# A twelfth cell and eight more key blocks of V 4 in the 15 KB that GpSimd's DMA scratch held

## The chip, the cores and the metric

The kernel runs on one core of one Trainium2 chip. The metric is the device time of one execution in microseconds, a median over runs. One core has a matrix engine (TensorE, PE in the profile, with PEld for its weight loads), VectorE (DVE), ScalarE (ACT), GpSimd (POOL), and SyncE (SP), which here only issues loads. Sixteen DMA engines move data from device memory (HBM) to the on-chip memory of 128 partitions (SBUF). TensorE writes to a second, smaller memory (PSUM).

## The reference: one token through two layers

One token of width 640 passes twice through the same pair of blocks: attention A over a cache of keys and values, and a small MLP B. Both passes read the same weights and, above all, the same two caches.

```python
x = A_x                                                    # [1, 1, 640]
for layer in range(2):
    x = x + A(layernorm(x), k_cache, v_cache, wq, wo)
    x = x + B(layernorm(x), w1, w2, w3, w4)

def A(x, k_cache, v_cache, wq, wo):                        # 32 heads of width 192
    q = (x @ wq) per head
    k, v = the last 4096 keys and values of the 32768 in each head's cache
    p = softmax(q @ k.T * 192 ** -0.5)
    return concat over heads (p @ v) @ wo

def B(x, w1, w2, w3, w4):
    x1 = x + (h = gelu(layernorm(x) @ w1), shifted by one or two tokens in four channel groups) @ w2
    return x1 + gelu(layernorm(x1) @ w3) @ w4
```

With one token every shift brings in zeros, so that w1 and w2 give nothing and B is the part with w3 and w4. All is bf16. One head's window of keys is 4096 x 192 x 2 B = 1536 KB, and so is that of its values: 32 heads, K and V, two layers make up nearly all that is moved.

## The kernel before

**Cells.** SBUF holds NCELL = 11 cells of 12,288 B in each of 128 partitions (FREE = 6144 bf16, 1536 KB in all). A cell takes one head's K window, one head's V window, a chunk of wo (four heads), or most of w3 or w4. `take` (L116) hands out the cell that was given back longest ago, `give` (L121) puts one at the end of the list. wq stays in SBUF for good. One order of loads, written out by `layer_stream` (L205) for each layer, is issued on SP's queue; `need` (L249) issues the loads up to the one that is asked for. A load waits on the queue until the cell that it was given is free, and all loads behind it wait too.

**One head.** K arrives with keys on partitions. VectorE transposes it in 32 x 32 blocks, in four quarters (`transpose_quart`, L360, the instruction is at L377), into a cell called the area, of which each quarter is reused; then TensorE computes the scores from the quarters (`scores`, L443, matmul at L453). When four heads (a group) have their scores, the softmax follows (`softmax_steps`, L473: part_max at L478 to recip at L533). Then P.V of the four heads, one after the other (`pv`, L560, matmul at L569), each followed by a transpose into o_sb (L576) and a fold (`o_fold`, L578). While one group is in P.V, the next one's K is transposed and its scores are computed. Layer 0 goes through the groups from the last (heads 28 to 31) to the first (0 to 3), layer 1 from the first to the last.

**What layer 0 keeps for layer 1.** Since both layers read the same caches, what stays on the chip needn't be loaded again:

- transposed keys of heads 0 to 6 (NKEEP = 7), each in a cell of its own taken at L369; layer 1 uses them without a load or a transpose, and gives the cell back after the head's scores (L664);
- V of head 3 (VC) in its cell;
- V of head 2 (VP): 20 of its 32 blocks wait in PSUM, into which and out of which VectorE transposes them (`v_words`, L550, at L558), the others in the cell of wo's chunk 0, which is kept too. In layer 1 head 2's V takes a cell, but has no load;
- of V of head 4 (VX) the last NKX = 6 of 32 key blocks, in a tile of their own, kx. A key block is 192 columns: one key per partition. In layer 1 the first 33 partitions of kx serve as row space after P.V of head 4 (L352, cleared at L853).

**Around the change of layers.** At the end of layer 0 seven cells hold kept keys, one V 3 and one wo chunk 0; two are left, through which w3 and w4 pass and then V 0 and V 1 of layer 1. The next cells come free only as layer 1 uses up kept heads: scores of heads 0 to 3 (L707), then those of 4 to 6 (L748), then the softmax of the first group, P.V of head 3, and only then the transposes and scores of head 7, whose K is the third load of layer 1. The load order of layer 1 is V 0, V 1, K 7, V 2 (no transfer), K 8, V 4, K 9, V 5, K 10 and so on. V 2's place in it is set at L233: behind the K of head NKEEP.

**The scratch.** The first 16 KB of each partition are set aside by the framework for descriptors of GpSimd's DMAs. The kernel issues no DMA from GpSimd.

The functions with the line numbers that the profile uses:

Of the kernel before, what the change touches and what calls it, by code (L numbers as in the profile page):

```python
# [8 lines left out]
BF16 = mybir.dt.bfloat16  # L9
# [8 lines left out]
P = 128  # L18
# [12 lines left out]

NJ4, NGK, NM = 4, 8, 4


@with_exitstack
def kernel(
# [12 lines left out]
    out: bass.AP,  # L49
):  # L50
    nc = tc.nc
    _, _, D = A_x.shape
    _, H, Sk, Dh = A_k_cache.shape
    W = min(4096, max(256, Sk // 4))
# [8 lines left out]
    QH = 4  # L63
# [5 lines left out]
    FREE = NT * QUART  # L69
# [2 lines left out]
    s0 = Sk - W  # L72

    NA = Dh // 32
    NKX = 6
    NKEEP, NCELL = 7, 11
    WARM = 4

    VC, VP, VX, VW, VN = 3, 2, 4, 20 * Dh // 2, NKX * Dh
    assert NA * D + FREE - 2 * VW <= FREE

    W3C, W4C = FREE // F, FREE // D
# [1 line left out]
    GROUPS = [[list(range(h, h + QH)) for h in range(0, H, QH)] for _ in range(2)]  # L86
    GROUPS[0].reverse()

    head = ctx.enter_context(tc.tile_pool(name="head", bufs=1))
    fixed = ctx.enter_context(tc.tile_pool(name="fixed", bufs=1))  # L90
    cells = ctx.enter_context(tc.tile_pool(name="cells", bufs=1))
# [11 lines left out]
        name=nc.get_next_instruction_name(), act_func_set_id=ACT_TABLE_SET, ins=[], outs=[]))  # L103
# [1 line left out]
    wq_sb = fixed.tile([P, ND, HD], BF16, name="wq_sb")  # L105
    wx_sb = fixed.tile([P, (ND - W3C) * F + (NF - W4C) * D], BF16, name="wx_sb")

    kx = fixed.tile([P, VN], BF16, name="kx")

# [4 lines left out]
    def take(key):  # L116
        i = free.popleft()
        cell_of[key] = i
        return cells.tile([P, FREE], BF16, tag=f"cell{i}", name=f"cell{i}")

    def give(key):  # L121
        free.append(cell_of.pop(key))
# [7 lines left out]
    def load_k(layer, h):  # L130
        t = take(("k", layer, h))
        nc.sync.dma_start(t[:], A_k_cache[0, h, s0:Sk, :].rearrange("(p j) d -> p (j d)", p=P))
        return t

    def load_v(layer, h):
        t = take(("v", layer, h))
        src = A_v_cache[0, h, s0:Sk, :].rearrange("(p j) d -> p (j d)", p=P)
        cut = (2 * VW,) if h == VP else (FREE - VN,) if h == VX else ()
        if h in GROUPS[layer][-1][-1 - layer:]:
            cut = FREE // 2,  # L140
        i = 0
        for e in cut + (FREE,):
            kept_v = h == VP or h == VX and i > 0
            if layer == 0 or not kept_v:
                nc.sync.dma_start(v_pair(t, h, i, e - i), src[:, i:e])
            i = e
        return t

    def v_pair(V, h, i, n):

        if h == VP and i >= 2 * VW:
            V, i = loaded["wo", 0, 0], i - 2 * VW + NA * D
        elif h == VX and i >= FREE - VN:
            V, i = kx, i - (FREE - VN)
        return V[:, i:i + n]

    def load_wq(layer, kc):
# [3 lines left out]
    def load_wo(layer, c):  # L161
        t = take(("wo", layer, c))
        src = A_wo[c * QC:(c + 1) * QC, :].rearrange("(p c) n -> p (c n)", c=NA)
        parts = {NG - 2: (3, 3), NG - 1: (3, 2, 1)}.get(c, (NA,)) if layer == 1 else (NA,)
        i = 0
        for n in parts:
            nc.sync.dma_start(t[:, i * D:(i + n) * D], src[:, i * D:(i + n) * D])
            i += n
        return t
# [13 lines left out]
    def load_w4(layer):  # L183
# [17 lines left out]
        return blocks  # L201

    LOADERS = {"x": load_x, "k": load_k, "v": load_v, "wq": load_wq, "wo": load_wo, "w3": load_w3, "w4": load_w4}

    def layer_stream(layer):  # L205
        groups = GROUPS[layer]
        seq, later = [], []

        def k_item(hh):
            if layer == 0 or hh >= NKEEP:  # L210
                seq.append(("k", layer, hh))

        def v_item(hh):
            if (layer, hh) == (1, VC):
                return
            if (layer, hh) == (1, VP):
                later.append(("v", layer, hh))
                return
            seq.append(("v", layer, hh))

        if layer == 0:
            for hh in groups[0]:
                k_item(hh)
        for gi, cur in enumerate(groups):
            nxt = list(groups[gi + 1]) if gi + 1 < len(groups) else []
            late = gi + 2 >= len(groups)
            for i, hh in enumerate(cur):
                if nxt:
                    k_item(nxt.pop(0))
                if nxt and late and i == 2:  # L230
                    k_item(nxt.pop(0))
                v_item(hh)
                if later and seq[-1] == ("k", layer, NKEEP):  # L233
                    seq.append(later.pop())
                if layer == 0 and gi + 1 == len(groups) and i < 2:
                    seq.append(("wo", layer, groups[gi + i - 1][0] // QH))
            if gi + 2 < len(groups) and gi >= layer:
                seq.append(("wo", layer, cur[0] // QH))
        if layer == 1:
            for g in groups[-2:]:  # L240
                seq.append(("wo", layer, g[0] // QH))
        seq.append(("w3", layer))
        seq.append(("w4", layer))
        return seq

    stream = [("wq", 0, 0), ("x",)] + [("wq", 0, kc) for kc in range(1, ND)] + layer_stream(0) + layer_stream(1)
    pos = [0]

# [311 lines left out]
    def pv(layer, h, hq, PT, mid=None):  # L560
        V = need("v", layer, h)
        if (layer, h) == (0, VP):
            v_words(0)
        NB = NJ4 * NGK // 2
        for i in range(NB):
            if mid is not None and i == NB // 2:
                mid()
            r = 32 * (i % 4)
            nc.tensor.matmul(O_ps[r:r + 2, :], lhsT=PT[:, hq, 2 * i:2 * i + 2],  # L569
                             rhs=v_pair(V, h, 2 * i * Dh, 2 * Dh), start=(i < 4), stop=(i >= NB - 4))  # L570
        if (layer, h) == (0, VC):
            loaded["v", 1, h] = V
            cell_of["v", 1, h] = cell_of.pop(("v", 0, h))
        else:
            give(("v", layer, h))
        nc.vector.transpose(o_sb[:], O_ps.rearrange("p (e a c) -> p e c a", e=2, c=NA))  # L576
# [426 lines left out]
```

## Time and profile before

| what | value |
|---|---|
| median of 3 runs | 519.34 us (519.17 to 519.5) |
| profiled execution, first to last instruction (span) | 517.8 us |
| median less span | 1.5 us |
| moved by DMA | 217.08 MB, 419 GB/s over the span |
| busy share: PE, DVE, ACT | 62%, 57%, 9% |
| K loads / whole V loads (1536 KB each) | 57 / 56 |
| mean granted TensorE clock | 0.697 of full speed |

Of the profiled execution the page gives the span alone: the time from its first instruction to its last. What an execution takes beside that isn't shown; the difference to the median of the runs is the estimate in the table.

How to read the lines in what follows: the page cuts the span into 40 slices of 12.9 us; a digit is the busy share in tenths, and GB/s is what the DMA engines moved in the slice. A timeline line has start and duration in us, engine, line of the kernel, operation, output <- inputs, shape, count of merged instructions, and in brackets the idle time of the engine before it and what ended that. SPq is SyncE's queue; its DMA lines are issues, and the data land later. A line of waits has the engine, its line and who ended the wait, then us in total, times, and the longest. A table of windows has a stretch, its length, the busy time of PE, PEld, DVE, ACT and POOL with counts, the granted TensorE clock, the DMA engines' busy share and GB/s.

### The profile page before, as it was taken

The numbers are of one execution on the slowest core, as the hardware profiler recorded it, in microseconds if no ns is written. First come the engines' busy times: TensorE is split into PE (matmuls) and PEld (weight loads), VectorE is DVE, ScalarE is ACT, GpSimd is POOL, SyncE is SP. The second block draws the span as 40 slices with busy tenths as digits, with TensorE's granted clock in tenths as the row PEclk, the third lists the DMA queues.
The fourth block names the chain that finished last, engine by engine and source line by source line (L and its number), as shares of the span: only waits on it lengthen the run. The fifth ranks groups of instructions, "written<-read, shape, count | busy, mean of one in ns | idle before, by whom it ended". The sixth has DMA issues, their size and how long they took to land.

```text
span 517.8 us, 9464 instructions
## 1 busy us (share of the span) xinstructions
PE 321.8 (62%) x4084; PEld 190.0 (37%) x4084; DVE 294.9 (57%) x591; ACT 48.9 (9%) x173; POOL 4.0 (1%) x16
## 2 busy tenths in 40 slices
PE   1057656666655655767755866668666667648665
PEld 0024333333332433434333634334333334425334
DVE  2067767575584764666624264756576766664722
ACT  1000101010010100001011001001010101001011
POOL 2000000000000000000000000000000000000000
PEclk9997778565585776677665567657787865776855
DMA  8999999999999999999999999999999999999996
GB/s 348 432 429 426 429 428 429 429 429 424 433 426 427 432 425 428 429 427 428 426 420 401 377 424 430 428 424 427 433 428 427 429 429 427 426 432 427 427 417 250
DMA packets 24093, 217.08 MB, mean 419 GB/s; under 512 B 2548, under 2 KB 3060, under 8 KB 8692
## 3 DMA queue, kind: packets, MB, share of 16 engines
q1 hardware_dynamic: 24052, 216.48, 99.0%
q8 instruction: 32, 0.52, 0.4%
q14 instruction: 9, 0.07, 0.0%
HBM read 216.47 MB, written 0.00 MB: 418 GB/s over the span
## 4 chain that ended last, share of the span: by engine, by line
DMA 50%; PE 23%; DVE 22%; issue 3%; ACT 1%; SPq 1%; DVEq 0%; ACTq 0%
DMA cell<-in_A_k_cache_dram 28%; DVE cell L377 16%; DMA cell<-in_A_v_cache_dram 16%; PE ST_ps L453 10%; PE O_ps L569 7%; DMA cell<-in_A_wo_dram 4%; DVE o_sb L576 2%; DMA cell<-in_B_w_dram 2%; DVE pm L478 1%; PE nb_ps L501 1%; DVE o_sb L512 1%; ACT o_sb L507 1%; PE l_ps L528 1%; PE PT_ps L523 1%; PE qT_ps L407 1%
## 5 line engine op out<-in xcount | busy, mean ns | idle before, releaser
L453 PE MATMUL ST_ps<-cell,Qblk 128*16 128x256 bf16 x1536 | 163.8, 383 | 108.2 <-DVE cell L377 70.1
L377 DVE STREAM_TRANSPOSE cell<-cell 128x768 uint32<-128x768 uint32 x228 | 204.0, 944 | 14.6 <-DMA cell<-in_A_k_cache_dram 14.3
L453 PEld LDWEIGHTS <-Qblk 128*16 128x16 bf16 x1536 | 85.8, 112 | 178.2 <-issue 151.0
L569 PE MATMUL O_ps<-cell,PT 128*2 128x384 bf16 x1018 | 98.7, 456 | 7.5 <-DMA cell<-in_A_v_cache_dram 5.5
L576 DVE STREAM_TRANSPOSE o_sb<-O_ps 128x384 f32<-128x384 f32 x64 | 37.1, 580 | 109.5 <-PE O_ps L569 109.4
L569 PEld LDWEIGHTS <-PT 128*2 128x2 bf16 x1024 | 45.6, 100 | 21.2 <-issue 11.4
L512 DVE STREAM_TRANSPOSE o_sb<-o_sb 128x256 bf16<-128x256 bf16 x16 | 7.1, 445 | 33.4 <-ACT o_sb L507 22.5
L584 ACT ACTIVATE oT<-oT_ps,rl 32x6 bf16<-32x6 f32 x40 | 10.3, 257 | 162.9 <-PE oT_ps L583 156.7
L583 PE MATMUL oT_ps<-o_sb,Lq 128*32 128x6 f32 x160 | 13.8, 195 | 10.4 <-DVE o_sb L576 9.9
L583 PEld LDWEIGHTS oT_ps<-o_sb,Lq 128*32 128x32 f32 x160 | 13.1, 145 | 19.4 <-issue 15.6
L589 ACT ACTIVATE oT<-oT_ps,rl 32x6 bf16<-32x6 f32 x24 | 6.2, 257 | 107.1 <-PE ST_ps L453 86.8
L407 PE MATMUL qT_ps<-xc,wq_sb 128*128 128x1 bf16 x210 | 7.2, 165 | 13.1 <-DMA wq_sb<-in_A_wq_dram 12.2
L523 PE MATMUL PT_ps<-o_sb,Eq 128*32 128x32 bf16 x256 | 7.2, 237 | 9.2 <-DVE o_sb L512 4.1
L421 DVE TENSOR_TENSOR Xq<-qT_ps,maskq 128x24 bf16<-128x24 f32 (+1 forms) x18 | 2.9, 159 | 17.4 <-PE qT_ps L407 17.4
L523 PEld LDWEIGHTS <-Eq 128*32 128x32 bf16 x256 | 5.4, 109 | 19.3 <-issue 19.2
L407 PEld LDWEIGHTS <-wq_sb 128*128 128x128 bf16 x210 | 6.8, 103 | 14.3 <-DMA wq_sb<-in_A_wq_dram 13.3
L504 ACT COPY nb_sb<-nb_ps 128x1 f32<-128x1 f32 x16 | 2.5, 159 | 96.2 <-PE nb_ps L501 96.2
L396 PE MATMUL qr_ps<-wq_sb,xc 128*1 128x384 bf16 x90 | 11.5, 398 | 0.0
L615 PE MATMUL yr_ps<-cell,oT 128*1 128x320 bf16 x108 | 10.8, 346 | 0.0
L528 PE MATMUL l_ps<-lh,ones 128*128 128x4 f32 x32 | 7.5, 306 | 4.9 <-ACT PT L526 4.9
L588 PE MATMUL oT_ps<-o,Lq 128*32 128x6 f32 x48 | 6.0, 198 | 6.5 <-DVE o L587 6.5
L428 PE MATMUL Qrep_ps<-Xq,Lb 128*128 128x24 bf16 (+1 forms) x18 | 3.2, 178 | 10.7 <-DVE Xq L421 10.4
(145 smaller groups left out, 196.7 us busy)
## 6 DMA issues: line engine op xcount, KB each, us to landing
cell<-in_A_k_cache_dram SPq DMA_DIRECT2D x57, 1536.0 KB, 25.2
cell<-in_A_v_cache_dram SPq DMA_DIRECT2D x56, 1536.0 KB, 25.3
cell<-in_A_wo_dram SPq DMA_DIRECT2D x13, 960.0 KB, 25.7
wq_sb<-in_A_wq_dram SPq DMA_DIRECT2D x5, 1536.0 KB, 12.5
cell<-in_A_v_cache_dram SPq DMA_DIRECT2D x6, 768.0 KB, 22.9
cell<-in_A_v_cache_dram SPq DMA_DIRECT2D x2, 1248.0 KB, 9.8
cell<-in_B_w_dram SPq DMA_DIRECT2D x1, 1536.0 KB
cell<-in_B_w_dram SPq DMA_DIRECT2D x2, 768.0 KB, 10.3
```

Of the source, the lines that this page charges most:

```text
L377: nc.vector.transpose(Tu, Ku[:, :, q * NY:(q + 1) * NY])
L396: nc.tensor.matmul(qr_ps[32 * i:32 * i + 1, :], lhsT=xc[:, kc:kc + 1], rhs=wq_sb[:, kc, t0 * P + i * N:t0 * P + (i + 1) * N], start=(kc == ...
L407: nc.tensor.matmul(qT_ps[:, tl:tl + 1], lhsT=wq_sb[:, kc, t * P:(t + 1) * P], rhs=xc[:, kc:kc + 1], start=(kc == 0), stop=(kc == ND - 1))
L453: nc.tensor.matmul(ST_ps[r:r + QW, :].rearrange("p (g i) -> p g i", g=ng), lhsT=Q[:, n, :], rhs=T4[:, :, f, :, t], start=(hq == 0 and n == ...
L512: nc.vector.transpose(held["PrT"], held["Pr"])
L523: nc.tensor.matmul(PT_ps[32 * m:32 * (m + 1), :, :, ng * q:ng * (q + 1)], lhsT=Eq[:, q, :], rhs=src[:, m:QW:NM], start=True, stop=True)
L528: nc.tensor.matmul(l_ps[:], lhsT=ones[:], rhs=held["lh"][:], start=True, stop=True)
L569: nc.tensor.matmul(O_ps[r:r + 2, :], lhsT=PT[:, hq, 2 * i:2 * i + 2], rhs=v_pair(V, h, 2 * i * Dh, 2 * Dh), start=(i < 4), stop=(i >= NB - 4))
L576: nc.vector.transpose(o_sb[:], O_ps.rearrange("p (e a c) -> p e c a", e=2, c=NA))
L583: nc.tensor.matmul(oT_ps[r, :], lhsT=Lq[:], rhs=o_sb[:, e, :, e], start=(e == 0), stop=(e == 1))
L584: nc.scalar.activation(oT[r, :], oT_ps[r, :], ACTF.Copy, scale=rl[r, 0:1])
L615: nc.tensor.matmul(yr_ps[32 * i:32 * i + 1, :], lhsT=oT[:, k:k + 1], rhs=wo_t[:, k * D + i * N:k * D + (i + 1) * N], start=(k == 0), stop= ...
```

## The change

The scratch is cut from 16 KB to 1 KB of each partition. In the 15 KB freed, a new pool `low` holds a twelfth cell (12,288 B) and a tile `kl` of 8 x 192 bf16 (3072 B). NKEEP becomes 8 and NCELL 12: head 7's transposed keys are kept too, and layer 1 has no load, no transposes and no area use for head 7; its scores are computed with those of heads 4 to 6 (L748). Of V 4 the last 14 key blocks are kept, 8 in kl and 6 in kx; layer 0 loads V 4 in three pieces, not two, and layer 1 loads its first 18 blocks, not 26. V 2's place in layer 1's order is now behind the last head of the first group: V 0, V 1, V 2 (no transfer), K 8, V 4, K 9 and so on. In layer 0 the area's cell is given back after head 11, no longer after head 7 (`last_plain`, L647).

```diff
+RING = 1024
+
+def shrink_ring(nc):
+    nc.dynamic_dma_scratch_size = RING
+    for a in nc.allocations:
+        for m in getattr(a, "memorylocations", ()):
+            if m.name == "DynamicDMAScratchLoc":
+                m.dims = [P, RING]
...
     nc = tc.nc
+    shrink_ring(nc)
...
-    NKX = 6
-    NKEEP, NCELL = 7, 11
+    NKX, NKL = 6, 8
+    NKEEP, NCELL = 8, 12
...
-    VC, VP, VX, VW, VN = 3, 2, 4, 20 * Dh // 2, NKX * Dh
+    VC, VP, VX, VW, VN = 3, 2, 4, 20 * Dh // 2, (NKL + NKX) * Dh
...
+    above, nc.sbuf_base = (nc.sbuf_base + 31) // 32 * 32, RING
+    low = ctx.enter_context(tc.tile_pool(name="low", bufs=1))
+    low.tile([P, FREE], BF16, tag=f"cell{NCELL - 1}", name=f"cell{NCELL - 1}")
+    kl = low.tile([P, NKL * Dh], BF16, name="kl")
+    low.seal()
+    nc.sbuf_base = above
...
-    kx = fixed.tile([P, VN], BF16, name="kx")
+    kx = fixed.tile([P, NKX * Dh], BF16, name="kx")
...
-        return cells.tile([P, FREE], BF16, tag=f"cell{i}", name=f"cell{i}")
+        return (low if i == NCELL - 1 else cells).tile([P, FREE], BF16, tag=f"cell{i}", name=f"cell{i}")
...
-        cut = (2 * VW,) if h == VP else (FREE - VN,) if h == VX else ()
+        cut = (2 * VW,) if h == VP else (FREE - VN, FREE - NKX * Dh) if h == VX else ()
...
+        elif h == VX and i >= FREE - NKX * Dh:
+            V, i = kx, i - (FREE - NKX * Dh)
         elif h == VX and i >= FREE - VN:
-            V, i = kx, i - (FREE - VN)
+            V, i = kl, i - (FREE - VN)
...
-                if later and seq[-1] == ("k", layer, NKEEP):
+                if later and i == QH - 1:
                     seq.append(later.pop())
```

## The prediction

> **What bounds the kernel now.** I read the page's slices and queues first, to see whether the DMA engines ever rest; then time windows around the one dip; then the order of issues there; then who waits for data afterwards.
>
> ```profile
> span 517.8 us, 9464 instructions
> ...
> DMA  8999999999999999999999999999999999999996
> GB/s 348 432 429 426 429 428 429 429 429 424 433 426 427 432 425 428 429 427 428 426 420 401 377 424 430 428 424 427 433 428 427 429 429 427 426 432 427 427 417 250
> ...
> q1 hardware_dynamic: 24052, 216.48, 99.0%
> ```
>
> The 16 DMA engines are busy for 99.0% of the span, at 424 to 433 GB/s in nearly every slice. Fewer bytes are the only large lever. The dip (401, 377) is the change of layers, at 283 to 297 us, where the change also works. There, in windows of 2 us (last two columns: DMA share, GB/s):
>
> ```profile
> 287.00:289.00 2.00, 1.48 (x33) 1.34 (x34) 0.51 (x5) 0.30 (x2) 0.00 (x0) 0.50 0.86 369
> 289.00:291.00 2.00, 1.70 (x36) 0.90 (x33) 0.35 (x3) 0.00 (x0) 0.00 (x0) 0.50 0.84 266
> 291.00:293.00 2.00, 2.00 (x31) 1.27 (x27) 0.21 (x1) 0.00 (x0) 0.00 (x0) 0.50 1.00 393
> ```
>
> Even here the engines idle only 0.14 and 0.16 of 2 us: 0.6 us. The timeline of that stretch shows why they idle at all: SyncE's queue (SPq) issues a load when a cell comes free, and cells come free one by one as PE finishes the scores (L453) of a kept head.
>
> ```profile
> 283.12 4.45 SPq L145 DMA_DIRECT2D cell<-in_A_v_cache_dram  x2
> ...
> 289.59 1.46 PE L453 MATMUL ST_ps<-cell,Qblk 128*16 128x256 bf16 x24 [0.30 <-DVE Qblk L436]
> ...
> 291.10 3.75 SPq L132 DMA_DIRECT2D cell<-in_A_k_cache_dram  x2
> ...
> 291.11 1.46 PE L453 MATMUL ST_ps<-cell,Qblk 128*16 128x256 bf16 x24
> ...
> 293.01 1.46 PE L453 MATMUL ST_ps<-cell,Qblk 128*16 128x256 bf16 x24
> ...
> 295.29 1.46 PE L453 MATMUL ST_ps<-cell,Qblk 128*16 128x256 bf16 x24
> ...
> 296.80 0.33 SPq L145 DMA_DIRECT2D cell<-in_A_v_cache_dram  x1
> ...
> 297.24 3.08 PE L453 MATMUL ST_ps<-cell,Qblk 128*16 128x256 bf16 x72 [0.35 <-DVE Qblk L436]
> ...
> 299.69 0.33 SPq L132 DMA_DIRECT2D cell<-in_A_k_cache_dram  x1
> ```
>
> V 0 and V 1 go out at 283.1 and 287.2. Kept head 0 ends at 291.05 and K 7 goes out at 291.10, into its cell. Head 1's cell goes to V 2, which has no transfer. Head 2's goes to K 8 (294.5), head 3's to V 4 (296.8), head 4's is the area, head 5's goes to K 9.
>
> After 300 us compute is behind the loads: from 300 to 480 us VectorE waits once for a K load, and PE only at the very end, after 500 us.
>
> ```profile
> DVE cell L377 <- DMA cell<-in_A_k_cache_dram: 1.9, 1, 1.9
> ```
>
> ```profile
> PE V_ps L901 <- DMA cell<-in_B_w_dram: 0.9, 1, 0.9
> PE y_ps L597 <- DMA cell<-in_A_wo_dram: 0.9, 2, 0.6
> ...
> PE O_ps L569 <- DMA cell<-in_A_v_cache_dram: 0.6, 1, 0.6
> ...
> PE y_ps L948 <- DMA cell<-in_B_w_dram: 0.2, 1, 0.2
> ```
>
> So on the way to the end compute has 1.9 + 2.6 = 4.5 us of waits for data, no more; what the loads gain beyond that compute must gain too.
>
> **The bytes.** Layer 1 no longer loads K 7 (1536 KB = 1.573 MB), and of V 4 it loads 18 blocks, not 26 (8 x 192 x 2 B x 128 = 384 KB = 0.393 MB). At the 428 GB/s of layer 1's slices that is 3.67 + 0.92 = 4.59 us. Layer 0 loads the same bytes as before.
>
> **Layer 0.** V 4 comes in three pieces, one issue more: 0.33 us on SP's queue, which there runs 13.1 us ahead (from issue to landing, the piece to kx). The slices with today's two pieces move 428 and 426 GB/s against 427 before them, so a further piece costs 0 to 0.1 us; I take 0.05. The Trainium skill speaks against the piece: "DMA: Bandwidth & Descriptors", section "Anatomy of one DMA", gives each DMA of GpSimd's path a fixed cost of some 2.0 us beside its bytes; if these loads paid it one after another, the gain would be 4.59 - 2.0 = 2.6 us. The trace doesn't bear that out: back-to-back loads run at 428 GB/s. Head 7's transposes (L377) go to a kept cell in place of the area: same instructions, no cost. The area comes free after head 11, not head 7, so at every point of the layer at least as many cells stream as before, and at its end two, as before. Some loads near 216 to 225 us wait for another release (K 0 for an earlier one; V 4 for P.V of head 9, not the transposes of head 6 just ahead of it, some 2 us), behind a queue of 13. Nothing. Layer 0 so ends when it did.
>
> **The change of layers: a gap.** Now the cell of kept head 0 goes to V 2, that of head 1 to K 8, of head 2 to V 4, head 3 the area, head 4 K 9, then V 5, K 10, V 6. The first transfer behind V 1 is K 8, issued at 291.11 + 1.46 = 292.6, where K 7 went at 291.1. V 1 lands at 287.2 + 8.1 (its time to landing) = 295.3; directly behind it K 8 would land at 295.3 + 3.7 = 299.0. Bounds from two rows: the first load of the kernel, into an empty queue, landed 6.4 us after its issue, and 292.6 + 6.4 = 299.0, no loss. V 1 itself, issued while V 0 ran out, took 8.1, and 292.6 + 8.1 = 300.7, a loss of 1.7 us. The 8.1 is nearer in place, but holds some waiting behind V 0, which isn't new; idle was 0.6 us in all around V 1. I take 0.6, and keep 0 to 1.7. V 4 (issued at 294.5) is not late. K 9 is due at 299.0 + 2.1 = 301.1 and issued at 297.24 + 1.03 to 1.46 = 298.3 to 298.7: between 0 and 0.3 more, I take 0. Below nothing the gap can't go: the queue was full before.
>
> **Compute in layer 1.** In the before, head 7's transposes and scores stood between P.V of heads 3 and 0: 3.51 us of VectorE from 307.07, P.V of head 0 at 311.9, the last o_sb (L576) of the group at 316.63. Now the scores of head 7 follow head 6 (a third of 3.08, 1.03 us, on PE; part_max and what hangs on it come 1.03 later), and the four P.V follow one another: from an o_sb at 306.56 + 1.03 = 307.6, three more at 1.7 us each (313.26, 314.92, 316.63 at full clock) to 2.4 (495.48, 497.86, 500.29 at 0.50). The last is at 312.6 to 314.8, so compute gains 1.8 to 4.0 us. Head 28's K landed at 462.2, compute was there 1.9 earlier, at 460.3; it now comes at 456.3 to 458.5, K 28 at 462.2 - 3.9 = 458.3. So the loads still bound, and behind that are 2.6 us more of waits. Later releases of cells come earlier too, and with 12 cells one load more can be under way: no new gap.
>
> **Sum.** 4.59 - 0.05 - 0.6 = 3.9 us off. The profiled span of 517.8 becomes 513.9; the 1.5 us between it and the median of 519.34 are outside the first and last instruction and stay: **515.4 us**. Its own range, by the gap's ends: 514.7 to 516.8.
>
> **Rivals.**
> *K 8 comes late in full.* Loss 1.7 + 0.3: 4.59 - 2.0 - 0.05 = 2.5 off, 516.8. For it: V 1's 8.1. Against it: only 0.6 us of idle engines then.
> *Compute becomes the bound.* From 317 to 462 no wait for data but one, so fewer bytes there buy only what compute gains. PE's granted clock was 0.60 to 0.82 by group; at 0.60 the group lasted from 317.14 to 346.42, 29.3 us. Five such, 146.5, against 143.2 now (317.14 to 460.3), lose 3.3. With the low gain of 1.8 and waits of 4.5: 1.8 + 4.5 - 3.3 = 3.0 off, 516.3. It decides once compute loses more than 2.4 us. Against it: no more work for PE.
> *More than forecast.* No gap, and full 4.6 off: 514.7, or a little under.
> *Slower: the scratch is needed after all.* If q1 kept its loads' descriptors in the 16 KB, 1 KB would hold a sixteenth. Late in layer 1 a load lands 27.8 us after its issue at 3.7 us each, so seven or eight are under way; two are enough to hide the 6.4 us of a lone one, and it decides below two: 216.48 MB / 1.573 = 138 loads x (6.4 - 3.7) = 370 us more, some 890. For it: nothing in the trace shows where descriptors lie. Against it: all issues are SP's, POOL has 16 instructions and no DMA. The Trainium skill, "DMA: Bandwidth & Descriptors", section "SWDGE vs HWDGE vs iDMA", puts the ring in SBUF for GpSimd's DMAs alone; by that rule this rival gives nothing lost, and the trace can't show it.
>
> **How the numbers follow.** Forecast 0.57, K 8 late 0.20, compute 0.10, more 0.03; within 0.2% (1.0 us, about what can be told from no change) 0.04, for both losses at ends further out than these rows; slower 0.06. Faster is 0.57 + 0.20 + 0.10 + 0.03 = 0.90. The range goes from 514.3 (the full 4.6, and 0.4 of today's 0.6 us of idle with it) to 517.2 (K 8 late, and 0.4 of the clock's loss).
>
> **What would show it.** K loads x56, not x57; bytes 217.08 - 1.97 = 215.1 MB; layer 0 the same to 283 us; the third load of layer 1 at 292.6 in place of 291.1, and one window there with less DMA share; no L377 near 307 us; the last o_sb of group 0 by 315 us; again a wait of L377 for a K near 458 us. I am wrong if a second dip appears after 300 us, if that wait for K is gone and the end comes with waits on PE alone, or if landings in layer 0 slow down.

## The result and the profile after

The changed kernel takes 515.82 us, median of four runs (515.72 to 515.96), the kernel before beside it 519.25 us (518.96 to 519.50). The ratio is 0.9934, with a 95% interval of 0.9920 to 0.9948. So 3.43 us came off, where 3.9 were forecast (515.4 us, range 514.3 to 517.2). The profiled execution took 515.88 us at a span of 514.1 us, 1.8 us apart; its mean granted TensorE clock was 0.669. The interval of the ratio allows 2.7 to 4.2 us, so 3.43 and 3.9 can't be told apart by this comparison alone.

In the new listing the lines have moved down: the transposes of K L377 are now L398, the scores L453 are L474, P.V L569 is L590, o_sb L576 is L597, the loads of K and V L132 and L145 are L151 and L164, and the matmuls of w3, w4 and wo (L901, L948, L597) are L922, L969, L618.

The page of the changed kernel first: span, the GB/s of the 40 slices, bytes, and the loads' queue (packets, MB, share of the 16 engines' time).

```profile
span 514.1 us, 9455 instructions
...
GB/s 348 432 429 428 429 428 429 427 428 428 429 431 428 429 424 430 432 423 430 427 420 415 344 409 430 429 425 428 427 431 427 429 427 431 427 428 431 429 413 251
DMA packets 24093, 215.11 MB, mean 418 GB/s; under 512 B 2548, under 2 KB 3060, under 8 KB 9076
...
q1 hardware_dynamic: 24052, 214.51, 99.0%
```

The bytes went from 217.08 to 215.11 MB as forecast, and the queue is as full as before (99.0%). Layer 0's slices are the same to within 5 GB/s. The dip at the change of layers is deeper: 415, 344, 409 GB/s where 401, 377, 424 stood. The same stretch of the changed kernel in 2-us windows (last three columns: granted TensorE clock, DMA share, GB/s):

```profile
287.00:289.00 2.00, 1.48 (x36) 1.34 (x34) 0.58 (x5) 0.30 (x2) 0.00 (x0) 0.50 0.88 371
289.00:291.00 2.00, 1.70 (x32) 0.89 (x29) 0.28 (x2) 0.00 (x0) 0.00 (x0) 0.50 0.81 289
291.00:293.00 2.00, 2.00 (x31) 1.28 (x34) 0.21 (x1) 0.00 (x0) 0.00 (x0) 0.50 0.92 381
293.00:295.00 2.00, 2.00 (x66) 1.54 (x69) 0.31 (x2) 0.46 (x2) 0.00 (x0) 0.91 0.87 301
295.00:297.00 2.00, 1.65 (x61) 1.18 (x53) 1.28 (x4) 0.00 (x0) 0.00 (x0) 1.00 0.96 356
```

The first three windows are near those of before (369, 266 and 393 GB/s). New are 293 to 297, with 301 and 356 GB/s where the kernel before moved 399 and 412:

```profile
293.00:295.00 2.00, 2.00 (x47) 1.28 (x47) 0.15 (x1) 0.46 (x2) 0.00 (x0) 0.50 1.01 399
295.00:297.00 2.00, 1.89 (x39) 1.07 (x36) 0.26 (x2) 0.00 (x0) 0.00 (x0) 0.50 0.97 412
```

SyncE's timeline in the changed kernel shows the issues behind it: V 0 and V 1, K 8, V 4, K 9; and the line's own view gives K 8's time to landing.

```profile
283.08 4.39 SPq L164 DMA_DIRECT2D cell<-in_A_v_cache_dram  x2
292.51 0.33 SPq L151 DMA_DIRECT2D cell<-in_A_k_cache_dram  x1
294.02 0.33 SPq L164 DMA_DIRECT2D cell<-in_A_v_cache_dram  x1
296.97 0.33 SPq L151 DMA_DIRECT2D cell<-in_A_k_cache_dram  x1
```

```profile
DMA to landing us min/median/max: 8.3/8.3/8.3
```

K 8 goes out 1.4 us later than K 7 did (291.10), because head 0's cell went to V 2, and lands at 292.51 + 8.3 = 300.8.

**A measure for the dip.** The DMA share does not say what the dip costs; the GB/s do. Sum (428 - GB/s) x 2 / 428 over the sixteen 2-us windows from 283 to 315 us: before 2.10 us, after 3.09 us. From 315 to 475 us the same sum is about zero in both (-0.02 and -0.07). So, up to 475 us, what is missing by 315 us is neither made up nor added to. I call this sum the shortfall. It is a rough measure: in two profiles of the changed kernel it is 3.09 and 2.73 us.

Compute in the changed kernel: the first and last o_sb of layer 1's first group, and the first transposes of head 28 (VectorE's timeline).

```profile
306.55 0.58 DVE L597 STREAM_TRANSPOSE o_sb<-O_ps 128x384 f32<-128x384 f32 x1 [1.14 <-PE O_ps L590]
...
313.70 0.58 DVE L597 STREAM_TRANSPOSE o_sb<-O_ps 128x384 f32<-128x384 f32 x1 [1.84 <-PE O_ps L590]
...
460.16 1.80 DVE L398 STREAM_TRANSPOSE cell<-cell 128x768 uint32<-128x768 uint32 x2
```

PE's waits for data from 300 us to the end (total us, times, longest):

```profile
PE V_ps L922 <- DMA cell<-in_B_w_dram: 1.1, 2, 0.9
...
PE y_ps L618 <- DMA cell<-in_A_wo_dram: 0.2, 1, 0.2
```

The group's last o_sb is 2.9 us earlier than before (316.63), yet head 28's transposes start at 460.16 without a wait: VectorE has no wait for a K load in this stretch at all. Waits for data fell from 1.9 + 2.6 us to 1.3 us. So at 460 us compute, not a load, was the later one, and compute is closer to being the bound than the forecast had it.

### The profile page after: what moved, and what is told of

Read it like the earlier page. It is cut to its first block, busy times and chain, and to the rows that moved or that the text cites. A ratio compares the mean times of both kernels' runs of the same rounds, so it can differ in the third digit from the quotient of the medians.

```text
span 514.1 us, 9455 instructions
## 1 busy us (share of the span) xinstructions
PE 325.7 (63%) x4084; PEld 190.2 (37%) x4084; DVE 291.2 (57%) x587; ACT 48.9 (10%) x173; POOL 4.0 (1%) x16
## 2 busy tenths in 40 slices
DMA packets 24093, 215.11 MB, mean 418 GB/s; under 512 B 2548, under 2 KB 3060, under 8 KB 9076
## 4 chain that ended last, share of the span: by engine, by line
DMA 54%; PE 23%; DVE 18%; issue 3%; ACT 1%; SPq 1%; DVEq 0%; ACTq 0%
DMA cell<-in_A_k_cache_dram 26%; DMA cell<-in_A_v_cache_dram 20%; DVE cell L398 13%; PE ST_ps L474 10%; PE O_ps L590 7%; DMA cell<-in_B_w_dram 4%; DMA cell<-in_A_wo_dram 4%; DVE o_sb L597 2%; PE qT_ps L428 1%; PE l_ps L549 1%; PE PT_ps L544 1%; PE nb_ps L522 1%; DVE pm L499 1%; DVE o_sb L533 1%; DVE V_ps L579 1%
## 5 line engine op out<-in xcount | busy, mean ns | idle before, releaser
L474 PE MATMUL ST_ps<-cell,Qblk 128*16 128x256 bf16 x1536 | 159.4, 375 | 104.9 <-DVE cell L398 68.4
L398 DVE STREAM_TRANSPOSE cell<-cell 128x768 uint32<-128x768 uint32 x224 | 200.4, 944 | 12.1 <-DMA cell<-in_A_k_cache_dram 11.8
L474 PEld LDWEIGHTS <-Qblk 128*16 128x16 bf16 x1536 | 83.7, 110 | 173.6 <-issue 147.5
L590 PE MATMUL O_ps<-cell,PT 128*2 128x384 bf16 x1010 | 101.3, 473 | 7.7 <-DMA cell<-in_A_v_cache_dram 5.6
L597 DVE STREAM_TRANSPOSE o_sb<-O_ps 128x384 f32<-128x384 f32 x64 | 37.2, 581 | 112.7 <-PE O_ps L590 112.6
L590 PEld LDWEIGHTS <-PT 128*2 128x2 bf16 x1024 | 46.2, 102 | 23.1 <-issue 14.6
L417 PE MATMUL qr_ps<-wq_sb,xc 128*1 128x384 bf16 x90 | 14.1, 468 | 0.0
L636 PE MATMUL yr_ps<-cell,oT 128*1 128x320 bf16 x108 | 12.3, 380 | 0.0
L522 PEld LDWEIGHTS nb_ps<-ones,o_sb 1*128 1x128 f32 x32 | 7.1, 275 | 7.2 <-issue 5.4
```

The lines of the kernel that those rows point to most:

```text
L398: nc.vector.transpose(Tu, Ku[:, :, q * NY:(q + 1) * NY])
L417: nc.tensor.matmul(qr_ps[32 * i:32 * i + 1, :], lhsT=xc[:, kc:kc + 1], rhs=wq_sb[:, kc, t0 * P + i * N:t0 * P + (i + 1) * N], start=(kc == ...
L474: nc.tensor.matmul(ST_ps[r:r + QW, :].rearrange("p (g i) -> p g i", g=ng), lhsT=Q[:, n, :], rhs=T4[:, :, f, :, t], start=(hq == 0 and n == ...
L522: nc.tensor.matmul(nb_ps[:], lhsT=held["w"], rhs=ones[0:1, 0:1], start=True, stop=True)
L636: nc.tensor.matmul(yr_ps[32 * i:32 * i + 1, :], lhsT=oT[:, k:k + 1], rhs=wo_t[:, k * D + i * N:k * D + (i + 1) * N], start=(k == 0), stop= ...
```

## The experiments

Three explanations for the part of 4.59 us that did not come were weighed: K 8's late issue (the loads bind and the gap is theirs); compute taking over as the bound; and the pieces of V 4 costing more than their bytes. The comparisons name the run's median, its range, and the ratio to the kernel before on the same chip.

**V 2 behind K 8.** The only edit gives head 0's cell to K 8 again.

```diff
-                v_item(hh)
-                if later and i == QH - 1:
+                if later and seq[-1] == ("k", layer, NKEEP):
                     seq.append(later.pop())
+                v_item(hh)
```

> The changed kernel with one edit of the load order: V 2, which takes a cell but has no transfer, stands behind K 8 and no longer ahead of it, so that K 8 takes the cell of kept head 0 and V 2 that of head 1. Nothing else is changed. Theory A (the changed kernel lost some 1 us of the bytes' gain because K 8, issued at 292.5 us, came late: it landed at 300.8, 1.7 us after the 299.0 at which it could): K 8 goes out at about 291.0, lands by 299.2 to 299.8, and the time falls by 0.7 to 1.2 us, to 514.6 to 515.1. Theory B (compute, not the loads, sets the end of the changed kernel; VectorE never waits for a K load any more): nothing is gained, 515.6 to 516.0, and the waits of PE for data at the end, 1.3 us in all, go to nearly nothing.

Measured: 514.76 us (514.58 to 516.08, four runs), ratio 0.9918 (0.9905 to 0.9932): 1.1 us better than the changed kernel. The profiled execution was the slowest of its four, and shows what can still go wrong. SyncE's issues of K 8, V 4, K 9, then PE's scores of heads 4 to 7, and two windows:

```profile
291.11 0.33 SPq L151 DMA_DIRECT2D cell<-in_A_k_cache_dram  x1
294.53 0.33 SPq L164 DMA_DIRECT2D cell<-in_A_v_cache_dram  x1
298.75 0.33 SPq L151 DMA_DIRECT2D cell<-in_A_k_cache_dram  x1
```

```profile
297.25 4.96 PE L474 MATMUL ST_ps<-cell,Qblk 128*16 128x256 bf16 x96 [0.35 <-DVE Qblk L457]
```

```profile
299.00:301.00 2.00, 2.00 (x44) 1.36 (x40) 0.48 (x2) 0.00 (x0) 0.00 (x0) 0.50 0.89 285
301.00:303.00 2.00, 1.47 (x33) 0.70 (x21) 0.42 (x1) 0.00 (x0) 0.00 (x0) 0.83 0.85 356
```

K 8 is in time, but the clock stayed at 0.50 until 301 us, head 4's scores ended late, and K 9, which waits for head 4's cell, opened the gap one load on. That the clock made this execution the slow one is argued from its trace; the other three have none. V 2 still holds a released cell ahead of a load that needs one.

**V 2 behind K 9.** The same edit with `NKEEP + 1`.

> The changed kernel, with V 2 (a cell, no transfer) placed two loads further back: V 0, V 1, K 8, V 4, K 9, V 2. K 8 takes the cell of kept head 0, V 4 that of head 1, K 9 that of head 2, V 2 that of head 3; VectorE needs V 2's cell only at about 296 us, when head 3's scores are done. With V 2 behind K 8 one execution of four took 516.08 against 514.6 to 514.8: in that one K 9 was issued at 298.75 us and landed 5.9 us after V 4, 2.2 more than its transfer. Theory A (late issues at the change of layers are the whole of what the change had lost): K 9 goes out near 294.5, no execution is above 515.0, and the median is 514.4 to 514.8. Theory B (compute binds beyond this): 514.7 at best, and the spread stays.

Measured: 514.57 us (514.43 to 514.95, four runs), ratio 0.9903 (0.9888 to 0.9919), 4.75 us off. Its issues of K 8, V 4, K 9, and the windows:

```profile
290.94 0.33 SPq L151 DMA_DIRECT2D cell<-in_A_k_cache_dram  x1
292.44 0.33 SPq L164 DMA_DIRECT2D cell<-in_A_v_cache_dram  x1
294.04 0.33 SPq L151 DMA_DIRECT2D cell<-in_A_k_cache_dram  x1
```

```profile
291.00:293.00 2.00, 2.00 (x31) 1.24 (x34) 0.21 (x1) 0.04 (x1) 0.00 (x0) 0.50 1.03 399
293.00:295.00 2.00, 2.00 (x66) 1.52 (x62) 0.30 (x2) 0.42 (x2) 0.00 (x0) 0.89 0.94 381
```

All of the 4.59 us is there, and no execution is above 514.95 us. The last 1.25 us are bought by the place of one entry, which loads nothing, in the order of cells. This version is the fastest that computes everything.

**K 8 later still.** In the changed kernel the area takes its cell right behind V 2, so that K 8 waits for head 2.

```diff
                     v_words(1)
+                    area[0] = take(("area", layer))
```

> The changed kernel with one thing more in K 8's way: layer 1's area, a cell that no load fills, is taken right behind V 2 and no longer after P.V of head 3. K 8 so gets the cell of kept head 2, V 4 that of head 3; K 9 that of head 4 as in the changed kernel. Theory A (the time follows the hour at which K 8 is issued: 291.0 us gave 514.6 to 514.8, 292.5 gave 515.8): K 8 is issued near 294.0, lands near 302.2, and the time is 516.9 to 517.5. Theory E (a late load is made up by the queue later, and the 1 us was something else about the order): 515.6 to 516.0.

Measured: 517.54 us (517.13 to 517.74, five runs), ratio 0.9958 (0.9943 to 0.9974): 1.7 us worse than the changed kernel. K 8's and K 9's issue, K 8's time to landing, and the gap:

```profile
294.34 0.33 SPq L151 DMA_DIRECT2D cell<-in_A_k_cache_dram  x1
...
298.57 0.33 SPq L151 DMA_DIRECT2D cell<-in_A_k_cache_dram  x1
```

```profile
DMA to landing us min/median/max: 6.2/6.2/6.2
```

```profile
293.00:295.00 2.00, 2.00 (x53) 1.35 (x45) 0.15 (x1) 0.41 (x2) 0.00 (x0) 0.50 0.33 131
295.00:297.00 2.00, 1.71 (x33) 0.90 (x29) 0.43 (x3) 0.00 (x0) 0.00 (x0) 0.50 0.88 233
```

The time came as expected, the step did not: K 8 landed at 300.5, no later than in the changed kernel (300.8). It found the queue nearly empty, 131 GB/s in the window of its issue. K 9 landed at 308.0, where it had landed at 306.6.

**The changed kernel again**, beside it:

> The changed kernel as it is, beside k8_later on the same chip: 515.7 to 516.0.

Measured: 516.02 us (515.65 to 516.84, four runs), ratio 0.9931 (0.9912 to 0.9950).

**The cell alone** (`NKX, NKL = 6, 0`, no kl; V 4 as before):

> The changed kernel without the eight more key blocks of V 4: scratch of 1 KB, the twelfth cell and the eighth kept head stay. Bytes saved against the kernel before: 1.573 MB, 3.67 us at 428 GB/s. Theory A (the missing 1 us is the gap at K 8, and comes with the eighth kept head): 3.67 - 0.9 to 1.1, a gain of 2.6 to 2.8 us, about 516.5. Theory C (the missing 1 us comes with the third piece of V 4 in layer 0, or its shorter load in layer 1): the full 3.67, about 515.6.

Measured: 516.70 us (516.10 to 517.97, five runs), ratio 0.9953 (0.9940 to 0.9965): 2.5 us of the 3.67 that K 7 weighs. So 1.2 us are missing without the pieces of V 4, and the third explanation falls.

**The blocks alone** (`NKEEP, NCELL = 7, 11`, kl stays):

> The changed kernel without the twelfth cell and the eighth kept head: scratch of 1 KB, eight more key blocks of V 4 kept. Bytes saved: 0.393 MB, 0.92 us; order of loads and cells as before the change. Theory A: no gap, a gain of 0.8 to 0.95 us, about 518.4. Theory C: the third piece eats it, 519.0 to 519.4.

Measured: 518.53 us (518.28 to 518.71, eleven runs), ratio 0.9985 (0.9976 to 0.9994): 0.66 us of 0.92. The two parts make 3.15 us, the whole 3.30 to 3.43: they add up to within 0.3 us.

**A spare cell** (`NKEEP, NCELL = 7, 12`: the blocks are kept, and the twelfth cell holds no kept head; it is one more for loads to pass through):

> The twelfth cell is there, but no eighth head is kept (seven as before), so that three cells, not two, stream at the change of layers; the eight blocks of V 4 are kept. V 0 of layer 1 can go out when P.V of head 2 of layer 0 is done, V 1 when w3 is used, K 7 when w4 is used, each one cell earlier. Bytes saved: 0.92 us. Theory A, that loads issued too late into a queue that runs empty are what the change of layers costs (about 0.9 us of idle engines and some 2 us of missing bytes between 283 and 304 us in the kernel before): the dip fills, a gain of 0.92 + 1 to 2 = 1.9 to 2.9 us, 516.4 to 517.4. Theory D, that the dip comes from small rows of the weights and engines out of step, not from late issues: 0.92 alone, 518.3.

Measured: 518.05 us (517.85 to 518.49, eleven runs), ratio 0.9978 (0.9969 to 0.9987): only 0.48 us beyond the blocks alone, a miss. Its windows, the two of the old dip, two behind it, and two at the end of the loads:

```profile
287.00:289.00 2.00, 1.48 (x36) 1.35 (x33) 0.57 (x5) 0.30 (x2) 0.00 (x0) 0.50 1.02 436
289.00:291.00 2.00, 1.70 (x35) 0.86 (x36) 0.28 (x2) 0.00 (x0) 0.00 (x0) 0.50 0.97 408
...
299.00:301.00 2.00, 1.38 (x41) 0.76 (x33) 0.79 (x3) 0.00 (x0) 0.00 (x0) 1.00 1.11 350
301.00:303.00 2.00, 1.18 (x32) 1.20 (x33) 0.55 (x3) 0.82 (x3) 0.00 (x0) 1.00 0.86 336
...
508.00:510.00 2.00, 1.00 (x38) 0.92 (x35) 0.15 (x1) 0.19 (x1) 0.00 (x0) 0.50 0.66 264
510.00:512.00 2.00, 0.82 (x32) 0.76 (x30) 1.34 (x11) 1.07 (x5) 0.00 (x0) 0.50 0.51 204
```

The old dip is filled (436 and 408 for 369 and 266 before); a new one opens at 299 us, where K 9 was issued only at 298.59. One more cell moves the shortage further on. By 315 us this kernel had moved 0.9 us' worth of bytes more than the blocks alone. But its loads did not land that much sooner: the first load of wo in layer 1 at 329.3 us (314.13 + 15.2) against 329.6 (313.78 + 15.8), the last load of all at 513.0 (issued at 503.34, 9.7 us to landing) against 513.3. The bytes that were ahead show up only at the end, as 264 and 204 GB/s where the blocks alone have 405 and 277. So bytes moved early are a gain only if the loads that compute needs land earlier. Why they did not here, the runs don't show. It also means that the dip of the kernel before, some 2 us, is not to be had whole by one earlier load.

The profiled executions together. The loss is the weight of the bytes saved less the gain, the gain from the median before on the same chip to the profiled execution:

| kernel | K 8 issued | shortfall, 283 to 315 us | its rise over 2.10 | loss |
|---|---|---|---|---|
| V 2 behind K 9 | 290.94 | 1.90 | -0.20 | 4.59 - 4.77 = -0.18 |
| V 2 behind K 8 | 291.11 | 3.30 | 1.20 | 4.59 - 3.11 = 1.48 |
| changed | 292.51 | 3.09 | 0.99 | 4.59 - 3.37 = 1.22 |
| changed, again | 292.44 | 2.73 | 0.63 | 4.59 - 3.48 = 1.11 |
| K 8 later still | 294.34 | 4.25 | 2.15 | 4.59 - 1.81 = 2.78 |
| cell alone | | 2.27 | 0.17 | 3.67 - 3.09 = 0.58 |
| blocks alone | | 1.92 | -0.18 | 0.92 - 0.76 = 0.16 |
| scratch alone (below) | | 1.93 | -0.17 | 0 - (-0.04) = 0.04 |
| spare cell | | 0.98 | -1.12 | 0.92 - 0.96 = -0.04 |

The rise of the shortfall and the loss go together to within some 0.6 us in all rows but the last, the spare cell, whose better filled windows brought no landing forward. The kernel before is one profile; the scratch alone, which loads the same, has 1.93 where that has 2.10, so a difference of 0.2 us says nothing.

**Is compute the bound?** From V 2 behind K 9, V 5 to 8 of layer 1 take eight blocks each from kl and load 0.393 MB less each (the matmuls read the tile all the same). This leaves out the right values of V for those blocks.

```diff
+    LESS = range(5, 9)
...
+        less = layer == 1 and h in LESS
+        if less:
+            cut = (FREE - VN, FREE - NKX * Dh)
...
+            kept_v = h == VP or h == VX and i > 0 or less and i == FREE - VN
```

> From v2_behind_k9: in layer 1 the V of heads 5 to 8 isn't loaded whole; blocks 18 to 25 of 32 are left out, and P.V reads those of head 4 in kl in their place. The result so is another; the same instructions run on PE, VectorE and ScalarE. 4 x 0.393 MB less, 3.67 us at 428 GB/s. Theory A (loads still bind): 514.6 - 3.67 + up to 0.2 for four more DMAs = 510.9 to 511.2. Theory B (compute is about to bind; it waited for data only 1.3 us in layer 1 of the changed kernel, and 4.2 us with V 2 behind K 8): less than half of it comes, 512.7 to 514.6, and no wait for K or V is left.

Measured: 511.51 us (511.42 to 512.81, four runs), ratio 0.9849 (0.9830 to 0.9868): 3.06 us less for 3.67 us of bytes less.

The same for V 5 to 29 (`LESS = range(5, 30)`), 23.0 us of loads less:

> As four_heads_less, but for heads 5 to 29 (all but the last two, which are loaded in halves): 25 x 0.393 MB = 9.8 MB less, 22.9 us. This asks where compute alone would end. By the waits for data seen from 300 us on (4.2 us with V 2 behind K 8): 510 to 511, since only those waits can go. If compute were also being held by cells that come late with the loads, lower: 505 or less.

Measured: 510.69 us (509.17 to 512.16, four runs), ratio 0.9827 (0.9800 to 0.9854). Its slices:

```profile
GB/s 347 429 431 428 428 426 431 426 431 427 431 428 425 429 429 429 429 426 427 427 423 418 369 407 429 424 427 422 424 427 425 425 426 421 425 425 422 413 79 3
```

The last load lands at 488.3 us (issued at 478.7, 9.6 us to landing), 21 us before the end, and nothing waits for data from 300 us on: this is what compute takes, some 510.7 us. In the kernel before and in all nine profiles of the table above, the last load lands some 3.3 us before the end of the span, so that the time moves with the loads. So at 515.8 the changed kernel is bound by loads, with about 5 us to go: 1.25 us came by the order of cells, then 3.06 us for 3.67 us of bytes. With four heads less the time is 0.3 us above the 510.9 to 511.2 expected for loads that still bind, which suggests that compute already takes a part there.

**The scratch alone.** The kernel before with the scratch cut to 1 KB and nothing put in its place:

> The kernel before with the scratch of GpSimd's DMAs cut to 1 KB and nothing put in its place. If the loads on SP's queue use nothing of it: no change, 519.0 to 519.4, and the time from issue to landing late in layer 1 stays at some 28 us. If their descriptors lay there: fewer loads under way, and a longer time.

Measured: 519.15 us (519.01 to 519.38, ten runs), ratio 0.9994 (0.9984 to 1.0003).

## Why the prediction was right, step by step

The time and the sign were right; the sum was 0.5 us too good, and the runs put that on one term, the gap at K 8.

- **Bytes, 4.59 us:** right. K loads x56, 215.11 MB, and V 2 behind K 9 brings all of it.
- **The further piece in layer 0, 0.05 us:** not contradicted. The blocks alone gained 0.66 us of 0.92, with an interval of 0.3 to 1.25 us, so the piece and all else on that side cost 0.26 us by the medians. The Trainium skill's fixed cost of about 2.0 us for each DMA ("DMA: Bandwidth & Descriptors", section "Anatomy of one DMA", told there of GpSimd's path), had it added up here, would by estimate have made that kernel 1.1 us slower than before; the interval excludes this.
- **Layer 0 unchanged:** right. V 0 is issued at 283.08, before at 283.12.
- **The gap at K 8, 0.6 us (0 to 1.7):** the mis-sized term, measured at 1.0 us of shortfall and 1.2 us of time in the profiled execution, and 1.25 us between the medians of the changed kernel and of V 2 behind K 9. K 8's issue came within 0.1 us of the forecast 292.6; its landing, 300.8, is the upper bound (8.3 us, by V 1's 8.1), not the middle. The step that failed is "idle was 0.6 us in all around V 1". That read the DMA share. By GB/s the same three windows of the kernel before (369, 266, 393) lack (59 + 162 + 35) x 2 / 428 = 1.2 us, and the whole stretch 2.1: at a share of 0.84 the engines moved 62% of their rate. So the argument that kept K 8 from its upper bound did not hold. Nor does K 8's landing settle the size: in the second profile of the changed kernel it was issued at 292.44 and landed 7.5 us later, at 299.9, only 0.9 us late, and the loss was 1.11 us all the same. That not all of the 1.7 showed may come from what the kernel before loses in these windows too; this is argued, not shown. What the times do follow is K 8's issue: at 290.9, 292.5 and 294.3 us it goes with 514.6, 515.8 to 516.0 and 517.5 us.
- **K 9, 0 us:** right in the profiled execution (issued at 296.97, its landing at 306.6 follows V 4's by one transfer). V 2 behind K 8 shows its price where the clock rises later.
- **Compute's gain, 1.8 to 4.0 us:** right, 2.9 us, with the last o_sb at 313.70 (forecast 312.6 to 314.8).
- **"Again a wait of L377 for a K near 458 us":** wrong. There was none. The last o_sb ahead of head 28 ended its wait at 459.66, where the kernel before had 459.74: the 2.9 us gained were gone again. The line of the kernel before:

```profile
459.74 0.58 DVE L576 STREAM_TRANSPOSE o_sb<-O_ps 128x384 f32<-128x384 f32 x1 [2.77 <-PE O_ps L569]
```

PE's granted clock in the changed kernel's third and fourth group shows where they went:

```profile
343.00:372.00 29.00, 21.22 (x236) 11.43 (x236) 17.92 (x35) 2.79 (x9) 0.00 (x0) 0.53 1.01 428
372.00:400.00 28.00, 19.83 (x211) 10.83 (x213) 18.55 (x34) 2.79 (x9) 0.00 (x0) 0.56 1.01 428
```

It was 0.53 and 0.56 here, below the 0.60 to 0.82 on which the forecast stood; the five groups took 460.16 - 314.20 = 146.0 us, against 143.2 before and 146.5 in the rival of compute. So that rival's premise came true, but not its result: the end still went with the loads. Here the forecast had some luck: compute lost 2.8 us, more than the 2.4 at which the rival was to decide, and did not only because its gain was 2.9 and not 1.8 (2.9 + 4.5 - 2.8 = 4.6 us, as much as the bytes). w3 and wo were waited for after 500 us, and V 2 behind K 9 shortened the kernel by another 1.25 us with no less work for PE.
- **The scratch:** the rival is refuted by its own run (0.9994). That agrees with the Trainium skill ("DMA: Bandwidth & Descriptors", section "SWDGE vs HWDGE vs iDMA"), which puts rings in SBUF only for GpSimd's DMAs.
- **The 1.5 us outside the span:** too small. In every profiled execution from the changed kernel on, time and span are 1.7 to 1.9 us apart. So the profile before, with its span of 517.8 us, came from an execution slower than the median of 519.34, and the 1.5 was too small by 0.2 to 0.4 us. Span to span 3.7 us came off, median to median 3.43.
- **The signs named for a failure:** no second dip after 300 us. In layer 0 the whole K and V loads took 27.8 us from issue to landing (median from 20 to 270 us), where the kernel before had 27.2 and 26.1. They did not arrive later for that, since V 0 of layer 1 is issued when it was and the slices move the same; with one more cell a load can be issued earlier and lie longer in the queue, which would give such figures. The wait for K did go, but the end did not come with waits on PE alone.

Open is why a load's time to landing into a draining queue varies between 6.2 and 8.7 us (8.3 and 7.5 for K 8 in two profiles of the same kernel), what sets the clock's course in one execution (by its trace, it made the gap in V 2 behind K 8's profiled one), and how the kernel before came to its own 2.1 us of shortfall beyond the late issues.

## What to carry to other kernels

Where the loads bind, price a gap by the bytes that its windows lack (rate of the full stretches less the rate there), not by the idle share of the DMA engines, and compare the sum before and after. Then look at when the next loads land: the spare cell's windows were fuller by 0.9 us than those of the blocks alone, but its first load of wo and its last load landed only 0.2 to 0.3 us sooner, and so the time barely moved. When buffers come free one by one, give the first to the load that goes out next; an entry that loads nothing can take the last. Memory freed is worth the loads that it removes, less what the order of its buffers spoils, and the second part was here some 1.2 us of 4.6.

## What the runs showed of the hardware

- DMA engines can count as busy while they move little: 0.87 of a window at 301 GB/s, 0.81 at 289, where full stretches have about 1.0 at 428.
- A 1536 KB load of 3.67 us landed 6.2 us after its issue with the queue nearly empty (K 8 later still), but 7.5 to 8.7 us after it into a queue that was running out (K 8 in the two profiles of the changed kernel 8.3 and 7.5, with V 2 behind K 9 8.6; K 9 with V 2 behind K 8 8.7).
- With the loads out of the way (25 heads less, V 2 behind K 9), one kernel took 509.17, 510.20, 511.17 and 512.16 us in four executions, at mean granted clocks of 0.718, 0.689, 0.666 and 0.682: the fastest has the highest clock, but the slowest not the lowest. This compute-bound version spreads over 3 us, where the load-bound ones spread over 0.24 (the changed kernel) to 1.9 us (the cell alone).
